# Scores from rounded parts and rests, softmax sums divided out of the rows of values, and the last layer's rows turned by DMA

## The chip, the core and the metric

The program runs on one core of a Trainium2 chip. The metric is device time in microseconds (us); lower is better. The engines are PE (TensorE, matrix products), DVE (VectorE), ACT (ScalarE), POOL (GpSimd) and SP, which here only starts transfers. Every engine takes its instructions strictly in the order in which the program lists them, and waits at the first one whose inputs or buffers are not there.

## What is computed

The reference, cut to what matters:

```
q, k, v: [4, 8, 576, 64]                      # batch, heads, rows, head size
scores = q @ k.T / 8;  keep the 32 largest of each row, others -> -1e9
attn = exp(scores - max) / (sum + 1e-9);      a = attn @ v
x = a as [2304, 512]                          # heads side by side
x = (sigmoid(x @ w_gate) * (x @ w_val)) @ w_out          # 512 -> 1536 -> 512
h = x @ w_in;  s = h * softmax(h)                        # 512 -> 1024
y = (s - mean(s)) / sqrt(var(s) + 1e-6) * g_ln @ w_out2  # 1024 -> 512
```

## The kernel before

**Chunks and steps.** The 2304 rows are handled as 18 chunks of 128 rows (16 of one batch, 2 that hold the remaining 64 rows of two batches each). A chunk has four steps, so there are 72; a step is one pair of heads (in the two remainder chunks two pairs of half the rows). The numbers behind tile names are steps or chunks: `ps40` is the score tile of step 40, `xt7` the input of chunk 7 to the layers.

**One step.** PE computes the scores in two halves of 288 keys (`scores`, L625 for the remainder, L628): fp32 products over 64 rows of the array, the two heads of the pair in the upper and the lower 64 rows. I call the instructions of one half a set: there are two sets a step. ACT takes them to SBUF (`s`, L634). DVE finds the 32nd largest value by rounds of MAX8 and MATCH_REPLACE8 (L639 to L657). ACT removes what lies below (L675) and takes the exponential with its row sum (L680). POOL and DVE make the inverse sum (L684, L688), ACT writes the normalized f16 part `h` with the inverse as a per-row scale (L701), POOL normalizes the fp32 values (`norm`, L693) and writes the f16 rest (L705). A DMA on SP's queue turns both parts (`et`, L712), and PE multiplies with the values (`attend`, tile `av`, L727).

**One chunk in the layers.** All products of the layers use three f16 terms: part by part, part by rest, rest by part. ACT writes the f16 part of the input (`xt`, L753); the rest comes either straight from DVE (`rows_direct`, L764, chunks in `DIRECT`), or by an fp32 copy on ACT and a difference on POOL (L771). PE then computes gate (`pg`) and value (`pv`, both L863), `px` (L909), `ph` (L946), after the normalization the turned rows (`pl`, L1018, eight fp32 transposes a chunk), and `po` (L1044). The part and the rest of `px` and `pl` are made as for `xt`, with `DIRECT` deciding for each chunk. The two chunks in `LATE` (16 and 17) have shorter ways at the end.

**The order.** A planner in the kernel (class `Order`) has a list of operations with engine, cost, due time, needs and buffers; due times are shifted by the table `SHIFT`. It plays the whole program once and writes out the order for every engine. Operations of different chunks and steps are thus interleaved: gate products of one chunk stand between score sets and `av` groups of later steps. At the start, weights are loaded (64-bit words from which DVE rebuilds fp32), summed, and split by ACT (L495, L496) and POOL (L499) into f16 part and rest. Buffers are counted by kind in `BUFS`: `pm` are the four PSUM tiles that all products of the layers share, `ps` the one score tile, `s` and `w` the step's SBUF tiles, `big` the two tiles for raw weights, `e` and `lt`.

Of the kernel before, what the change touches and what calls it, by code (L numbers as in the profile page):

```python
# [1189 lines left out]
```

## Time and profile before

| | |
|---|---|
| median of 3 runs | 1003.15 us (1002.62 to 1004.39) |
| the profiled execution | 1002.34 us |
| its span, first to last instruction | 1000.6 us |
| PE busy | 883.0 us, 88% |
| DVE busy | 865.0 us, 86% |
| ACT busy | 724.4 us, 72% |
| POOL busy | 569.6 us, 57% |

The profile is of one execution. The start of a PE instruction is recorded, its end is modelled, so the time a group of matmuls holds PE is read from the distance to the next group's start, and not from the duration beside it. Durations on ACT and DVE overlap their neighbours by about 0.1 us.

### The profile page before, as it was taken

The numbers are of one execution on the slowest core, as the hardware profiler recorded it, in microseconds if no ns is written. First come the engines' busy times: TensorE is split into PE (matmuls) and PEld (weight loads), VectorE is DVE, ScalarE is ACT, GpSimd is POOL, SyncE is SP. The second block draws the span as 40 slices with busy tenths as digits, with TensorE's granted clock in tenths as the row PEclk, the third lists the DMA queues.
The fourth block names the chain that finished last, engine by engine and source line by source line (L and its number), as shares of the span: only waits on it lengthen the run. The fifth ranks groups of instructions, "written<-read, shape, count | busy, mean of one in ns | idle before, by whom it ended". The sixth has DMA issues, their size and how long they took to land.

```text
span 1000.6 us, 29578 instructions
## 1 busy us (share of the span) xinstructions
PE 883.0 (88%) x12052; PEld 668.1 (67%) x12052; DVE 865.0 (86%) x2321; ACT 724.4 (72%) x1319; POOL 569.6 (57%) x824
## 2 busy tenths in 40 slices
PE   1343249899999999999999999999999999999995
PEld 1112138777786868786877777676868687877962
DVE  7999999999999999999899999999999999823232
ACT  4998999888789878667797776777987677632221
POOL 6876787786657766555475645645673546530000
PEclk9999658999999999999999999999999999999998
DMA  9982565142641433332514433334332224220000
GB/s 339 327 257 66 138 158 126 30 83 65 141 118 38 95 85 58 82 93 75 112 51 76 63 59 84 84 82 106 77 73 61 69 49 83 50 59 4 10 12 21
DMA packets 194200, 91.56 MB, mean 92 GB/s; under 512 B 171792, under 2 KB 181008, under 8 KB 194064
## 3 DMA queue, kind: packets, MB, share of 16 engines
q1 hardware_dynamic: 194064, 89.68, 36.7%
q8 instruction: 94, 1.54, 0.7%
q14 instruction: 42, 0.34, 0.1%
HBM read 42.47 MB, written 4.72 MB: 47 GB/s over the span
## 4 chain that ended last, share of the span: by engine, by line
PE 75%; DVE 13%; ACT 6%; DMA 3%; issue 1%; POOL 1%; SPq 0%; POOLq 0%; ACTq 0%; DVEq 0%
PE pg L863 15%; PE pv L863 14%; PE px L909 12%; PE ph L946 9%; PE po L1044 9%; PE ps L628 8%; PE av L727 6%; DVE m L653 3%; DVE w L657 2%; PE pl L1018 2%; DVE pd L424 1%; DMA raw<-in_w_in_dram 1%; DMA wi<-in_w_gate_dram 1%; DVE pd L427 1%; PE ps L625 1%
## 5 line engine op out<-in xcount | busy, mean ns | idle before, releaser
L653 DVE MAX8 m<-w 128x8 f32<-128x288 f32 (+1 forms) x576 | 328.6, 598 | 0.1
L657 DVE MATCH_REPLACE8 w<-m,w 128x288 f32<-128x288 f32 (+1 forms) x432 | 232.5, 542 | 0.0
L705 POOL TENSOR_TENSOR h<-s,h 128x576 f16<-128x576 f32 x144 | 184.5, 1285 | 3.1 <-POOL nk L662 0.2
L863 PE MATMUL pg<-xt,wg 128*128 128x128 f16 x2592 | 180.1, 222 | 3.2 <-POOL xt L771 2.2
L909 PE MATMUL px<-gh,wo 128*128 128x128 f16 x2592 | 177.7, 219 | 0.0
L863 PEld LDWEIGHTS <-wg 128*128 128x128 f16 x2592 | 158.1, 100 | 22.9 <-issue 12.1
L863 PE MATMUL pv<-xt,wv 128*128 128x128 f16 x2592 | 171.9, 219 | 0.1
L909 PEld LDWEIGHTS <-wo 128*128 128x128 f16 x2592 | 152.0, 98 | 23.0 <-issue 13.4
L863 PEld LDWEIGHTS <-wv 128*128 128x128 f16 x2592 | 152.5, 98 | 20.5 <-issue 9.9
L693 POOL TENSOR_SCALAR s<-s,sm 128x576 f32<-128x576 f32 x144 | 106.7, 745 | 102.2 <-ACT h L701 101.7
L628 PE MATMUL ps<-k,q 64*128 64x288 f32 x512 | 105.3, 488 | 28.9 <-ACT s L634 11.7
L634 ACT ACTIVATE s<-ps 128x576 f32<-128x576 f32 x144 | 92.6, 643 | 50.6 <-PE ps L628 38.0
L675 ACT ACTIVATE s<-s,nk 128x576 f32<-128x576 f32 x144 | 105.3, 767 | 32.5 <-POOL nk L662 32.3
L701 ACT ACTIVATE h<-s,sm 128x576 f16<-128x576 f32 x144 | 107.4, 767 | 20.4 <-DVE sm L688 16.6
L1044 PE MATMUL po<-wo,lt 128*128 128x512 f16 x432 | 119.7, 389 | 0.0
L946 PE MATMUL ph<-wi,x 128*128 128x512 f16 x432 | 119.5, 388 | 0.0
L680 ACT ACTIVATE s<-s,nb 128x576 f32<-128x576 f32 x144 | 110.0, 766 | 1.1 <-POOL nb L669 1.0
L628 PEld LDWEIGHTS ps<-k,q 64*128 64x128 f32 x512 | 42.1, 198 | 67.8 <-issue 21.4
L727 PE MATMUL av<-et,v 128*64 128x128 f16 (+1 forms) x2400 | 77.9, 220 | 6.5 <-ACT v L608 6.0
L727 PEld LDWEIGHTS <-v 128*64 128x64 f16 x2400 | 66.3, 113 | 23.9 <-issue 12.7
L639 DVE TENSOR_TENSOR w<-ps,s 128x576 f32<-128x576 f32 x72 | 54.1, 751 | 26.1 <-ACT s L634 17.5
L684 POOL TENSOR_SCALAR sm<-sm 128x2 f32<-128x2 f32 x72 | 13.8, 191 | 108.9 <-ACT s L680 103.7
(166 smaller groups left out, 1236.9 us busy)
## 6 DMA issues: line engine op xcount, KB each, us to landing
v<-in_v_pad_dram SPq DMA_DIRECT2D x16, 320.0 KB, 4.1
k<-in_k_dup_dram SPq DMA_DIRECT2D x32, 144.0 KB, 3.1
wi<-in_w_gate_dram SPq DMA_DIRECT2D x8, 512.0 KB, 6.0
q<-in_q_main_dram SPq DMA_DIRECT2D x32, 128.0 KB, 3.3
wo<-in_w_val_dram SPq DMA_DIRECT2D x8, 512.0 KB, 7.6
wi<-in_w_out_dram SPq DMA_DIRECT2D x8, 512.0 KB, 5.4
raw<-in_w_in_dram SPq DMA_DIRECT2D x8, 512.0 KB, 4.8
raw<-in_w_out_dram SPq DMA_DIRECT2D x8, 512.0 KB, 4.4
```

Source lines behind the costliest of these rows:

```text
L628: nc.tensor.matmul(ps[:, t, :S // 2], q[rows, p], kv["k", b, p][rows, keys], start=True, stop=True)
L653: nc.vector.max(st["m8"][:, t, r * 8:r * 8 + 8], ranked(i, r, t))
L657: nc.vector.match_replace(w, steps[i]["m8"][:, t, r * 8:r * 8 + 8], w, LOW)
L680: nc.scalar.activation(w, w, AF.Exp, bias=st["nb"][:, t:t + 1], scale=D ** -0.5, accum_out=st["sm"][:, t:t + 1])
L693: nc.gpsimd.tensor_scalar(w, w, st["sm"][:, t:t + 1], 1.0, op0=OP.mult, op1=OP.mult)
L701: nc.scalar.activation(st["h"][:, 0, t], st["s"][:, t], AF.Copy, scale=st["sm"][:, t:t + 1])
L705: nc.gpsimd.tensor_sub(st["h"][:, 1, t], st["s"][:, t], st["h"][:, 0, t])
L727: nc.tensor.matmul(ch["av"][j * D:(j + 1) * D, p, st["o"]:st["o"] + wd], v, e[:, y * REM:y * REM + wd], start=one and k == (0, 5)[j], stop ...
L863: nc.tensor.matmul(dst, w[a][:, c, f * P:(f + 1) * P], ch["xt"][:, b, c], start=x == 0, stop=x == len(mm) - 1)
L909: nc.tensor.matmul(ch["px"][:, e], wo1h[a][:, f, e * P:(e + 1) * P], ch["gh"][:, b, f], start=y == 0, stop=y == len(DOWN) - 1)
L946: nc.tensor.matmul(ch["ph", nn], ch["x2"][:, a, c], wih[b][:, c, nn * 512:(nn + 1) * 512], start=c == 0 and a == 0 and b == 0, stop=c == K ...
L1044: nc.tensor.matmul(ch["po"], ch["lt"][:, a, f], wo2h[b][:, f], start=y == 0, stop=y == len(FIN) - 1)
```

## The change

- **Scores.** `q` and `k` are split when loaded: a part rounded to float32r (F32R; ACT, `split_q`, `split_k`) and the rest (POOL, `rest_q`, `rest_k`). The `k` tile of one head holds the rounded part in 64 of its rows and the rest in the other 64, and `q` stands in both halves, so that one F32R product over 128 rows gives part by part and part by rest. A second F32R product over 64 rows adds rest by part. A set has four matmuls in place of two (eight in place of four in the remainder). `k` is loaded with both copies, `q` once a step and not once a chunk.
- **Softmax sums.** `h` is written from the exponentials without a scale, and `norm` is gone. The inverse sums are made once a chunk, split in two f16 parts (`inverse_halves`), spread over the array by PE (`spread`, tile `rb`, 16 matmuls a chunk, 32 in a remainder chunk), taken to SBUF by ACT (`take_spread`) and multiplied with `av` by DVE (`rows_all`). From this ACT makes the part of `xt`, POOL the rest.
- **Last layer.** For the chunks 0 to 15 ACT and POOL split the rows into part and rest (`last_hi`, `last_lo`) and one DMA turns both (`flip_last`); the PE transposes and the three ways of making `lt` from `pl` stay for chunks 16 and 17.
- **Tables.** `DIRECT` holds chunks 16 and 17 only, so the rest of `px` is made by ACT and POOL for the others. `BUFS` and `SHIFT` are new, and with them the order.

```diff
-DIRECT = tuple(range(4, 18))
+DIRECT = (16, 17)
-BUFS = dict(s=4, ks=5, v=4, q=2, w=4, et=2, ...)
+BUFS = dict(s=3, ks=8, v=4, qr=2, qs=3, w=3, et=2, ...)
     ("w", "g"): -850.7, ...
+    ("w", "g"): -600.6, ...
+    def split_q(i):
...
+        nc.scalar.activation(st["qh"], st["qr"], AF.Copy)
+    def rest_q(i):
...
+            nc.gpsimd.tensor_sub(st["ql"][rows, :n], st["qr"][rows, part], st["qh"][rows, part].bitcast(F32))
+    def split_k(b, p, j):
...
+        nc.scalar.activation(ks, kv["raw", b, p, j], AF.Copy)
+    def rest_k(b, p, j):
...
+        rows = slice(D - j * D, P - j * D)
+        nc.gpsimd.tensor_sub(ks[rows], kr[rows], ks[rows].bitcast(F32))
@@ scores
-                    nc.tensor.matmul(ps[:, t, :S // 2], q[rows, p], kv["k", b, p][rows, keys], start=True, stop=True)
+        for x, p in enumerate(st["pairs"]):
+            for t in range(2):
+                nc.tensor.matmul(ps[:, t, :S // 2], qh[:, t * num + x], kv["k", b, p, t][:, keys], start=x == 0, stop=False)
         for x, p in enumerate(st["pairs"]):
             for t in range(2):
                 rows = slice(t * D, t * D + D)
+                nc.tensor.matmul(ps[:, t, :S // 2], ql[rows, x], kv["k", b, p, t][rows, keys], start=False, stop=x == num - 1)
-    def norm(i, t):
...
+    def spread(ch):
+        ch["rb"] = rb = tl(pp, [P, NPAIR, P], F32, f"rb{ch['x']}", "pm")
+        for y, i in enumerate(ch["steps"]):
...
+                for a in range(2):
+                    for t in range(2):
+                        nc.tensor.matmul(rb[t * D:t * D + D, p, st["o"]:st["o"] + wd], ch["ih"][:, a, 2 * y + t:2 * y + t + 1].to_broadcast([P, D]),
+                                         ident16[:, rows], start=a == 0, stop=a == 1)
@@ prob_hi
-        nc.scalar.activation(st["h"][:, 0, t], st["s"][:, t], AF.Copy, scale=st["sm"][:, t:t + 1])
+        nc.scalar.activation(st["h"][:, 0, t], st["s"][:, t], AF.Copy)
+    def take_spread(ch):
...
+            nc.scalar.activation(ch["xf"][:, :, w], ch["rb"][:, :, w], AF.Copy, scale=by)
     def rows_all(ch):
+        nc.vector.tensor_mul(ch["xf"], ch["av"], ch["xf"])
     def rows_hi(ch):
+        nc.scalar.activation(ch["xt"][:, 0], ch["xf"], AF.Copy)
+    def last_hi(ch):
...
+        nc.scalar.activation(ch["lh"][:, 0], ch["e"].rearrange("p a b -> p (a b)"), AF.Copy)
+    def last_lo(ch):
+        nc.gpsimd.tensor_sub(ch["lh"][:, 1], ch["e"].rearrange("p a b -> p (a b)"), ch["lh"][:, 0])
+    def flip_last(ch):
+        nc.sync.dma_start(ch["lt"].rearrange("p c k q -> p (c k) q"), ch["lh"].rearrange("p c f -> p (c f)"), transpose=True)
```

**Where the order moves, first place.** PE in the middle of the program, before: the end of a gate group, four of the eight transposes of a chunk, a score set, and the start of an `av` group.

```order
L863 LDWEIGHTS wg_75
L863 MATMUL pg_7940<-xt7_7464,wg_75 128x128
L1018 MATMUL pl_8045<-ident_64,e_7786 128x128 x4
L628 MATMUL ps37_1_8052<-k2_1_6849,q9_0_6630 128x288 x2
L727 LDWEIGHTS v1_2_4356
L727 MATMUL av32_7565<-et34_7871,v1_2_4356 64x128
```

PE now, the same score set: its four matmuls stand between value products.

```order
L899 MATMUL pv_8571<-xt7_7872,wv_78 128x128
L647 MATMUL ps37_1_8590<-ks2_1_0_7818,qs37_7824 128x288
L647 MATMUL ps37_1_8590<-ks2_1_1_7956,qs37_7824 128x288
L651 MATMUL ps37_1_8590<-ks2_1_0_7818,qs37_7824 128x288
L651 MATMUL ps37_1_8590<-ks2_1_1_7956,qs37_7824 128x288
L899 LDWEIGHTS wv_78
```

The transposes are gone from this place, and the set has two matmuls over the whole array (L647) ahead of two over half of it (L651). Before, two fp32 instructions stand there, each of which the trace shows as two records.

**Second place.** ACT ahead of the input of chunk 1 (`xt1`), before: splitting of weights, then `xt1` straight from `av`.

```order
L496 ACTIVATE wo2_79<-wo2_79,gscale_81 128x512
L495 ACTIVATE ts_2112<-wo2_79,gscale_81 128x512
L496 ACTIVATE wo2_79<-wo2_79,gscale_81 128x512
L753 ACTIVATE xt1_2129<-av4_1737 128x512
L675 ACTIVATE s9_1730<-s9_1730,nk9_2039 128x576
```

ACT now at this place.

```order
L791 ACTIVATE xf_2263<-rb1_2154 128x512
L706 ACTIVATE s8_1925,sm8_2261<-s8_1925,nb8_2230 128x576
L738 ACTIVATE h8_2301<-s8_1925 128x576
L657 ACTIVATE s10_2307<-ps10_0_2240 128x2x288
L497 ACTIVATE ts_2320<-wo2_81,gscale_83 128x512
L498 ACTIVATE wo2_81<-wo2_81,gscale_83 128x512
L738 ACTIVATE h8_2301<-s8_1925 128x576
L798 ACTIVATE xt1_2330<-xf_2263 128x512
```

`xt1` now stands behind work of step 8 and behind the spread sums of its own chunk (`xf` from `rb1`); between that row and `xt1` DVE has to multiply.

## Rows read from the trace of the kernel before

**Rows 1.** Waits of PE from 200 to 960 us, all of them: total, times, longest

```profile
PE ps L628 <- DVE w L643: 1.1, 2, 0.8
PE ptot L385 <- ACT sq L915: 0.8, 1, 0.8
PE pg L863 <- ACT ot L1051: 0.4, 1, 0.4
PE pl L1018 <- POOL e L1013: 0.2, 1, 0.2
```

**Rows 2.** Busy time by stage: stretch, length, PE, PEld, DVE, ACT, POOL, clock, DMA

```profile
150.00:200.00 50.00, 46.37 (x714) 41.25 (x710) 48.25 (x126) 44.08 (x75) 37.74 (x50) 0.91 0.33 78
200.00:350.00 150.00, 147.75 (x2224) 112.75 (x2222) 142.87 (x405) 125.61 (x238) 105.37 (x155) 1.00 0.41 90
350.00:850.00 500.00, 499.71 (x7010) 376.89 (x7010) 476.74 (x1318) 376.15 (x703) 286.43 (x453) 1.00 0.35 76
```

**Rows 3.** Timeline of PE in two places: start, us, what, [wait]

```profile
452.98 0.84 PE L946 MATMUL ph<-wi,x 128*128 128x512 f16 x3
453.75 0.76 PE L628 MATMUL ps<-k,q 64*128 64x288 f32 x4
454.44 0.85 PE L946 MATMUL ph<-wi,x 128*128 128x512 f16 x3
...
462.69 0.84 PE L946 MATMUL ph<-wi,x 128*128 128x512 f16 x3
463.45 1.03 PE L727 MATMUL av<-et,v 128*64 128x128 f16 x30
464.42 0.85 PE L909 MATMUL px<-gh,wo 128*128 128x128 f16 x12
```

**Rows 4.** The same view around a remainder set and a gate group

```profile
243.94 0.83 PE L863 MATMUL pg<-xt,wg 128*128 128x128 f16 x12
244.70 0.72 PE L625 MATMUL ps<-k,q 64*64 64x288 f32 x8
245.35 0.84 PE L863 MATMUL pg<-xt,wg 128*128 128x128 f16 x12
246.03 0.84 PE L1044 MATMUL po<-wo,lt 128*128 128x512 f16 x3
```

**Rows 5.** The same view around four of the transposes

```profile
862.40 0.61 PE L1018 MATMUL pl<-ident,e 128*128 128x128 f32 x4
862.84 0.83 PE L863 MATMUL pg<-xt,wg 128*128 128x128 f16 x12
```

**Rows 6.** Groups of ACT, POOL and DVE: line, what, count | busy us, mean ns | idle before

```profile
L701 ACT ACTIVATE h<-s,sm 128x576 f16<-128x576 f32 x144 | 107.4, 767 | 20.4 <-DVE sm L688 16.6 <-issue 2.4 <-ACT s L634 0.9
L894 ACT ACTIVATE gh<-sg 128x512 f16<-128x512 f32 x54 | 32.3, 621 | 19.1 <-DVE sg L889 18.8
L693 POOL TENSOR_SCALAR s<-s,sm 128x576 f32<-128x576 f32 x144 | 106.7, 745 | 102.2 <-ACT h L701 101.7
L705 POOL TENSOR_TENSOR h<-s,h 128x576 f16<-128x576 f32 x144 | 184.5, 1285 | 3.1 <-POOL nk L662 0.2
L764 DVE SCALAR_TENSOR_TENSOR lt<-pl,lt 128x512 f16<-128x512 f32 x28 | 19.0, 683 | 25.0 <-ACT lt L1023 25.0
```

**Rows 7.** Chain that ended last, where chunk 0 enters the layers: start, us, what

```profile
145.07 0.43 ACT xt L753
...
150.70 7.16 PE pg L863 x84
```

**Rows 8.** The same view, where chunk 1 enters

```profile
188.17 0.88 ACT wo L496
189.05 0.44 ACT xt L753
...
190.72 1.16 POOL xt L771
...
191.93 3.10 PE pg L863 x38
```

More of the change, by code (lines that the diff above doesn't have):

```diff
@@ L11 @@
 F32 = mybir.dt.float32
+F32R = mybir.dt.float32r
 F16 = mybir.dt.float16
@@ L44 @@
 V_DOWN = 11
-BUFS = dict(s=4, ks=5, v=4, q=2, w=4, et=2, ps=1, pt=1, av=1, pm=4, xt=1, gh=1, two=3, big=2, xf=1, x2=1)
+BUFS = dict(s=3, ks=8, v=4, qr=2, qs=3, w=3, et=2, ps=1, pt=1, av=1, pm=4, xt=1, gh=1, two=3, big=2, xf=1, x2=1)
 STEP = 12.0
@@ L173 @@
                 POOL=(100, 70, 80, 100, 1250), DMA=(0,) * 5)
-    TAKER = dict(s="ACT", ks="DMA", v="DMA", q="DMA", w="DVE", et="DMA", ps="PE", pt="PE", av="PE", pm="PE",
+    TAKER = dict(s="ACT", ks="ACT", v="DMA", qr="DMA", qs="ACT", w="DVE", et="DMA", ps="PE", pt="PE", av="PE", pm="PE",
                  xt="ACT", gh="ACT", two="ACT", big="DMA", xf="ACT", x2="ACT")
@@ L538, in weights @@
             W = (key, f, c)
-            add(("wh", *W), "ACT", 1.48, t + 0.6 * x, lambda f=f, c=c: split_hi(f, c), [("wc", key)], take=["two"])
+            add(("wh", *W), "ACT", 1.44, t + 0.6 * x, lambda f=f, c=c: split_hi(f, c), [("wc", key)], take=["two"])
             add(("wl", *W), "POOL", 1.23, t + 0.6 * x, lambda f=f, c=c: split_lo(f, c), [("wh", *W)], free=["two"])
@@ L572, in body @@
         ch["x"] = x
+        ch["steps"] = [i for i, st in enumerate(steps) if st["ch"] is ch]
     kv = {}
@@ L576, in body, with load_q, load_k @@
     vstat = cp.tile([P, B * NPAIR], F32, name="vstat")
-    def load_q(ch, j):
-        ch["q", j] = qt = tl(sp, [P, NPAIR, P], F32, f"q{ch['x']}_{j}", "q")
-        b = ch["vs"][j]
+    def load_q(i):
+        st = steps[i]
+        if st["rem"]:
+            st["qr"] = tl(sp, [P, 4, P], F32, f"qr{i}", "two")
+            nc.sync.dma_start(st["qr"], q_rem[st["b"], st["c"]])
+        else:
+            st["qr"] = tl(sp, [P, 2, P], F32, f"qr{i}", "qr")
+            p = 2 * st["pairs"][0]
+            nc.sync.dma_start(st["qr"], q_main[st["b"], st["c"], :, p:p + 2])
+    def split_q(i):
+        st = steps[i]
+        st["ql"] = qs = tl(sp, [P, 3, P], F32R, f"qs{i}", "qs")
+        st["qh"] = tl(sp, [P, 4, P], F32R, f"qh{i}", "two") if st["rem"] else qs[:, 1:]
+        nc.scalar.activation(st["qh"], st["qr"], AF.Copy)
+    def rest_q(i):
+        st = steps[i]
+        n = len(st["pairs"])
         for t in range(2):
             rows = slice(t * D, t * D + D)
-            if ch["rem"]:
-                nc.sync.dma_start(qt[rows].rearrange("d (h x) q -> d h x q", h=2),
-                                  q_rem[b, :, rows, 2 * t:2 * t + 2].rearrange("h d x q -> d h x q"))
-            else:
-                nc.sync.dma_start(qt[rows], q_main[b, ch["c"], rows].rearrange("d (p j) q -> d p j q", j=2)[:, :, t])
-    def load_k(b, p):
-        kv["k", b, p] = kt = tl(sp, [P, S], F32, f"k{b}_{p}", "ks")
-        for t in range(2):
-            nc.sync.dma_start(kt[t * D:t * D + D], k_dup[b, 2 * p + t, t * D:t * D + D])
+            part = slice(t * n, t * n + n)
+            nc.gpsimd.tensor_sub(st["ql"][rows, :n], st["qr"][rows, part], st["qh"][rows, part].bitcast(F32))
+    def load_k(b, p, j):
+        kv["raw", b, p, j] = kr = tl(sp, [P, S], F32, f"kr{b}_{p}_{j}", "big")
+        nc.sync.dma_start(kr, k_dup[b, 2 * p + j])
+    def split_k(b, p, j):
+        kv["k", b, p, j] = ks = tl(sp, [P, S], F32R, f"ks{b}_{p}_{j}", "ks")
+        nc.scalar.activation(ks, kv["raw", b, p, j], AF.Copy)
+    def rest_k(b, p, j):
+        kr, ks = kv["raw", b, p, j], kv["k", b, p, j]
+        rows = slice(D - j * D, P - j * D)
+        nc.gpsimd.tensor_sub(ks[rows], kr[rows], ks[rows].bitcast(F32))
     def load_v(b, p):
@@ L778, in body @@
         t = use[0] * STEP
-        add(("kd", b, p), "DMA", 1.0, t - 3 * STEP, lambda b=b, p=p: load_k(b, p),
-            ([("kd", b, p - 1)] if p else [("kd", b - 1, NPAIR - 1)] if b else []), take=["ks"], delay=0.95)
+        for j in range(2):
+            add(("kd", b, p, j), "DMA", 0.85, t - 3 * STEP, lambda b=b, p=p, j=j: load_k(b, p, j),
+                ([("qk", uses[b - 1, p][-1], 1)] if b else []) + [("kd", b, p, 0)] * j, take=["big"], delay=0.95)
+            add(("kb", b, p, j), "ACT", 0.575, t - 2 * STEP,
+                lambda b=b, p=p, j=j: split_k(b, p, j), [("kd", b, p, j)], take=["ks"])
+            add(("ka", b, p, j), "POOL", 1.37, t - 2 * STEP, lambda b=b, p=p, j=j: rest_k(b, p, j),
+                [("kb", b, p, j)], free=["big"])
         add(("vd", b, p), "DMA", 0.91, t - STEP, lambda b=b, p=p: load_v(b, p), take=["v"], delay=0.95)
@@ L786, in body @@
             add(("vl", b, p, x), "POOL", 0.75, t + STEP, lambda b=b, p=p, x=x: value_lo(b, p, x), [("vh", b, p, x)], free=["two"])
-    for x, ch in enumerate(chunks):
-        ch["steps"] = [i for i, st in enumerate(steps) if st["ch"] is ch]
-        for j in range(len(ch["vs"])):
-            add(("qd", x, j), "DMA", 0.8, ch["steps"][2 * j] * STEP - 3 * STEP, lambda ch=ch, j=j: load_q(ch, j),
-                [("qd", x, j - 1) if j else ("qd", x - 1, len(chunks[x - 1]["vs"]) - 1)] if x or j else [], take=["q"], delay=0.95)
     for i, st in enumerate(steps):
@@ L795, in body @@
         rem, b, ch = st["rem"], st["b"], st["ch"]
-        done_q = st["last"] or rem and ch["steps"].index(i) == 1
+        add(("qd", i), "DMA", 0.8 if rem else 0.5, t0 - 3 * STEP, lambda i=i: load_q(i), [("qd", i - 1)] * (i > 0) + [("qk", i - 1, 1)] * rem,
+            take=["two" if rem else "qr"], delay=0.95)
+        add(("qb", i), "ACT", 0.52 if rem else 0.31, t0 - 2 * STEP, lambda i=i: split_q(i), [("qd", i)] + [("qb", i - 1)] * (i > 0),
+            take=["qs"] + ["two"] * rem)
+        add(("qa", i), "POOL", 1.4 if rem else 0.78, t0 - 2 * STEP, lambda i=i: rest_q(i), [("qb", i)], free=["two" if rem else "qr"])
         for n in range(2):
-            add(("qk", i, n), "PE", 0.5, t0 - STEP, lambda i=i, n=n: scores(i, n),
-                [("qd", ch["x"], st["j"])] + [("kd", b, p) for p in st["pairs"]] + ([("qk", i, 0)] if n else [("qk", i - 1, 1)] if i else []), take=["ps"],
-                free=(["q"] * done_q + ["ks"] * sum(uses[b, p][-1] == i for p in st["pairs"])) * n)
-            add(("se", i, n), "ACT", 0.53, t0 - STEP, lambda i=i, n=n: take_scores(i, n), [("qk", i, n)] + [("se", i, 0)] * n,
+            add(("qk", i, n), "PE", 0.95 if rem else 0.5, t0 - STEP, lambda i=i, n=n: scores(i, n),
+                [("qa", i)] + [("ka", b, p, t) for p in st["pairs"] for t in range(2)] + ([("qk", i, 0)] if n else [("qk", i - 1, 1)] if i else []),
+                take=["ps"], free=(["qs"] + ["two"] * rem + ["ks"] * sum(2 * (uses[b, p][-1] == i) for p in st["pairs"])) * n)
+            add(("se", i, n), "ACT", 0.55, t0 - STEP, lambda i=i, n=n: take_scores(i, n), [("qk", i, n)] + [("se", i, 0)] * n,
                 take=["s"] * (n == 0), free=["ps"] * (n == 0))
@@ L820, in body @@
         for t in range(2):
[L821 removed]
+            add(("be", i, t), "ACT", 0.68, e, lambda i=i, t=t: below(i, t), [("nk", i), ("se", i, 1)])
             add(("ex", i, t), "ACT", 0.76, e, lambda i=i, t=t: expo(i, t), [("be", i, t), ("nb", i)])
[L823 to L824 removed]
         for t in range(2):
[L826 to L828 removed]
+            add(("hh", i, t), "ACT", 0.6, e, lambda i=i, t=t: prob_hi(i, t), [("ex", i, t)] + [("hh", i, 0)] * t + [("hh", i - 1, 0)] * (t == 0 and i > 0), take=["w"] * (t == 0))
+            add(("hl", i, t), "POOL", 1.28, e, lambda i=i, t=t: prob_lo(i, t), [("hh", i, t)] + [("hl", i, 0)] * t,
                 free=["s"] * t)
[L830 removed]
+        add(("tr", i), "DMA", 3.5, e + 3, lambda i=i: flip_halves(i), [("hl", i, 1)] + [("tr", i - 1)] * (i > 0), take=["et"], free=["w"], delay=1.5,
             room=lambda i=i: room_halves(i))
@@ L849, in body @@
                     needs.append(("vk", key, bb))
-            cost = 0.57 if len(ch["vs"]) == 1 else 0.8
-            add(("xh", ch["x"]), "ACT", cost, e + 6, lambda ch=ch: rows_hi(ch), needs, take=["xt"])
-            if ch["x"] in DIRECT:
-                add(("xl", ch["x"]), "DVE", 0.6 if len(ch["vs"]) == 1 else 0.75, e + 6, lambda ch=ch: rows_direct(ch), [("xh", ch["x"])], free=["av"])
-            else:
-                add(("xf", ch["x"]), "ACT", cost, e + 6, lambda ch=ch: rows_all(ch), [("xh", ch["x"])], take=["xf"], free=["av"])
-                add(("xl", ch["x"]), "POOL", 1.11, e + 6, lambda ch=ch: rows_rest(ch), [("xf", ch["x"])], free=["xf"])
+            x = ch["x"]
+            add(("iw", x), "POOL", 0.19, e, lambda ch=ch: total1(ch), [("ex", y, t) for y in ch["steps"] for t in range(2)])
+            add(("iv", x), "DVE", 0.08, e, lambda ch=ch: inverse(ch), [("iw", x)])
+            add(("ih", x), "POOL", 0.36, e, lambda ch=ch: inverse_halves(ch), [("iv", x)])
+            add(("rb", x), "PE", 0.46, e + 5, lambda ch=ch: spread(ch), [("ih", x)] + ([("va", x - 1, 7)] if x else []), take=["pm"])
+            add(("rs", x), "ACT", 0.5 if len(ch["vs"]) == 1 else 0.7, e + 5, lambda ch=ch: take_spread(ch), needs[1:] + [("rb", x)], take=["xf"], free=["pm"])
+            add(("xa", x), "DVE", 0.61, e + 6, lambda ch=ch: rows_all(ch), [("at", i), ("rs", x)], free=["av"])
+            add(("xh", x), "ACT", 0.52, e + 6, lambda ch=ch: rows_hi(ch), [("xa", x)], take=["xt"])
+            add(("xl", x), "POOL", 1.12, e + 6, lambda ch=ch: rows_rest(ch), [("xh", x)], free=["xf"])
     def group(ch, dst, w, f):
@@ L1063, in tA, with op @@
             return (4 * x + BEHIND + 4 * a / ATOMS) * STEP
-        def op(name, engine, cost, a, fn, needs=(), take=(), free=(), table=None, delay=0.0, x=x, port=None):
-            add((*name[:1], x, *name[1:]), engine, cost, tA(a), fn, needs, take, free, table, delay, port)
+        def op(name, engine, cost, a, fn, needs=(), take=(), free=(), table=None, delay=0.0, x=x, port=None, room=None):
+            add((*name[:1], x, *name[1:]), engine, cost, tA(a), fn, needs, take, free, table, delay, port, room)
         if ("fs", key) not in order.ops:
@@ L1119, in body @@
         N = ATOMS
-        for nn in range(2):
+        if x not in LATE:
+            op(("lh",), "ACT", 0.95, 57, lambda ch=ch: last_hi(ch), [("l4", x)], take=["w"])
+            op(("ll",), "POOL", 2.3, 57, lambda ch=ch: last_lo(ch), [("lh", x)], free=["big"])
+            op(("lr",), "DMA", 3.1, N + 10, lambda ch=ch: flip_last(ch), [("ll", x)], take=["big"], free=["w"], delay=1.5,
+               room=lambda ch=ch: room_last(ch))
+        for nn in range(2) if x in LATE else ():
             op(("tu", nn), "PE", 0.455, N + 22, lambda ch=ch, nn=nn: turn(ch, nn), [("l4", x)], take=["pm"],
```

69 lines of the change are left out of this document (31 added, 38 removed), and 137 rows, old and new, of the table SHIFT.

## The prediction

> **What bounds the kernel now.** I read the waits of PE first. From 200 to 960 us PE waited for other engines four times, 2.5 us in all [rows 1]. So in that stretch the time is the sum of what PE has to do. The stages beside it [rows 2] show how little that says about the others: from 350 to 850 us DVE is busy 476.7 of 500 us (95%), ACT 376.2 (75%), POOL 286.4 (57%), and yet none of them is waited for. From 150 to 200 us it is different: PE is busy only 46.4 of 50 us, ACT 44.1, DVE 48.3. In the chain [rows 7, 8] the first gate product of chunk 0 starts at 150.70 after ACT's `xt`, and that of chunk 1 at 191.93, after ACT has split weights until it comes to `xt` at 189.05. So the program is: start until 150.7, ACT in front of chunk 1, then PE alone until the last chunk. A saving of PE counts in full; a saving of DVE counts for nothing as long as PE is not waiting; more work on ACT counts in the first 200 us, and later only if it eats ACT's idle quarter.
>
> **PE's prices.** What a group holds is read from starts. A group of 1536 f16 columns (12 matmuls of 128, 3 of 512) holds PE 0.68 us (245.35 to 246.03, [rows 4]), so 128 columns cost 0.057 and 288 columns 0.127. A score set: 452.98 to 453.75 is 0.77, 0.09 more than the group ahead of it needs, and 453.75 to 454.44 is 0.69 [rows 3]; the set costs 0.78. Four fp32 transposes cost 0.44, 0.11 each with its own weights [rows 5], that is 0.25 for 288 fp32 columns. The trace counts four records a set, two upper, two lower, side by side; two of 0.25 one after the other make 0.50, and 0.28 is left for entering and leaving the half-array form. An `av` group of 30 matmuls in 15 side-by-side pairs costs 0.08 ahead plus 0.97 [rows 3], 1.05; 15 x 0.057 leave 0.20 for entering and leaving.
>
> **The change on PE.**
> - Sets, 128 of them in the main steps: two full-array matmuls and one side-by-side pair, 3 x 0.127 + 0.28 = 0.66 against 0.78, so -0.12 x 128 = -15.4 us. Here is the one open price: no row shows an F32R matmul. Below it is bounded by the f16 rate, 0.127, above by the fp32 rate, 0.25 for 288 columns. I take 0.127, since an f16 operand and a rounded one are both a single part, and the two records of fp32 are what several parts cost. By "FP8 and Floating Point Precision" of the Trainium skill (TensorE Precision Notes) full fp32 is four products of halves; one of four would be an estimated 0.125 and move the sum by 1 us.
> - Remainder sets, 16: now 0.09 + 0.65 = 0.74 (243.94 to 244.70 to 245.35, [rows 4]); then four full ones and two pairs, 6 x 0.127 + 0.28 = 1.04. +0.30 x 16 = +4.8 us.
> - Transposes of 16 chunks: 128 x 0.11 = -14.1 us.
> - `rb`: 16 matmuls, 8 pairs, 8 x 0.057 + 0.20 = 0.66 for 16 chunks; at most twice that for the two remainders, I take 0.75. +12.0 us.
>
> Sum -12.7 us. Some sets stand directly behind one another before and pay the way in once, which gives back about 1. Of what is left some 2.5 fall before the first gate, where PE waits anyway: the sets of the first steps are in the order of either kernel ahead of it. **On the path: -9 us.**
>
> **The other engines.** DVE loses 24 differences for `lt`, 12 for `px`, about 14 for `xt` at 0.68 each [rows 6] and most reciprocals, and gains 18 multiplications: about -30 us, worth nothing by rows 1, but it gives DVE room. POOL loses `norm`, 144 x 0.745, and gains the rests of `q`, `k`, `xt`, `px` and the last rows, about as many elements, but as differences (1.285 for 576 against 0.745, [rows 6]): some +50 us on an engine with 43% idle. ACT gains the roundings of `q` (64 of 256 elements) and `k` (32 of 576), the last layer's part and more copies of `px`; it loses the copies of `pl` and the per-row scale of `h`. From 0.621 for 512 elements [rows 6] I estimate 0.33 for 256 and 0.70 for 576 without the scale, against 0.767 with it: about +45 us in all, 2.5 a chunk. In 350 to 850 us that fits into the idle quarter. A wait is added on SP: the turning of the last rows waits for POOL, and behind it in SP's queue stand loads of `q` and `k` and the turning of later steps' `h`. What is late then is an `av` group; the planner keeps these some us ahead of PE, and I give it 1 us together with the tighter last step, whose score set is now about 24 us of PE work ahead of its `av` group, where it was 32.
>
> **The start.** Ahead of `xt0` ACT's queue now has 8 roundings of `q` (2.6), 8 of `k` (5.6) and one spread copy (0.6) more, and two exponentials, two removals, one `h` and two pieces of weight splitting less, with the cheaper `h` about 6: +2.8, and with 0.1 us of overlap for each of the net 10 instructions +1.8. After `xt` the way is shorter: 145.07 to 150.70 now has a second copy in a queue; then it is ACT 0.62, POOL 1.16 [rows 8] and three hand-overs, about 2.3 against 5.6. First gate: 150.7 + 1.8 - 3.3 = 149.2.
>
> **Chunk 1.** Ahead of `xt1` the same count gives +13.4 us (12 roundings of `q`, 8 of `k`, four instructions of one more step, three on `px` of chunk 0, the rest cancels), less overlap for 27 instructions: +10.7. The way from `xt1` to the gate is 0.6 shorter. ACT's idle time in 150 to 200 us, 5.9 us [rows 2], can take some of it or none: gate of chunk 1 between 191.93 + 10.7 - 0.6 - 5.9 = 196.1 and 202.0, I take 199.5. PE would be there at 149.2 + 41.5 (its work by these prices up to there, 35 before) + 3.8 (the same excess as before, 189.5 less 150.7 less 35) = 194.5. So PE waits 5 us, and ACT decides.
>
> **The sum.** From chunk 1's gate to the end the trace has 1000.6 - 191.9 = 808.7 us. Of PE's work 6.5 us have moved in front and 9 are gone: 808.7 - 15.5 = 793.2. End: 199.5 + 793.2 + 2 (SP, the last step, ACT now and then) = 994.7. The profiled execution took 1.7 us more than its span, and lies 0.8 below the median: **997 us**, about 0.5% faster than 1002.3.
>
> **Rivals.**
> - *ACT stays late.* Up to `xt4` ACT's queue grows by about 16 us. If its idle time (24 of 150 us from 200 to 350, [rows 2]) lies where ACT waits for others and none of it is taken up, chunk 4 comes 16 us late, and the 15.5 us that PE saves behind are eaten: 1000.6 + 0.5 + 2 + 1.7 = 1005, with more such places up to 1012. It decides from the point where PE waits over 10 us in front of chunks 1 to 4. For it: ACT is in the chain at both entries [rows 7, 8]. Against: from chunk 2 on ACT is not waited for [rows 1]. 0.23.
> - *The weights of the rounded matmuls load in the open.* A load of 128 fp32 columns takes at most the 0.11 of a transpose [rows 5]; 320 full-array matmuls x 0.11 = +35 us: 1032. At the fp32 rate the 480 places of a matmul or pair would cost 0.12 more, +58: 1050 with ACT's wait gone. For it: no row shows F32R. Against: transposes with their own fp32 weights follow every 0.11, less than one 0.127. The Trainium skill says in "TensorE: Matmul & The Clock Gate" (Part 3, what overlaps and what doesn't) that a weight load overlaps a running matmul only when the row group differs; by that rule 1032. The trace disagrees for f16: twelve matmuls, each with its own weights for the same rows, hold PE 0.68 us [rows 4]; no run here shows it for F32R. 0.10.
> - *DVE sets the pace after all*, 95% busy as it is, and PE's order only follows: then its -30 us count, 972 to 985. Against: rows 1. 0.10.
>
> **How the numbers follow.** Forecast 0.57, around 997, by itself 988 to 1004 (ACT's idle time taken up or not, +-3; a step of 0.02 in the F32R matmul, +-8; SP and the order). The others as given. The range leaves out the slow matmuls and half of the DVE case: 984 to 1012. A measurement here can tell about 0.2%, 2 us, from no change. Faster: 0.70 of the forecast and the DVE case, 0.50; same: 0.16, from the forecast's upper end and the lower end of the ACT case; slower: 0.34.
>
> **What would show it.** PE's score set: starts 0.66 us apart from the group behind it beyond its own lead (right), near 0.9 (open loads) or over 1.0 (fp32 rate). No `pl` before chunk 16; `rb` groups of 0.66. First gate near 149, chunk 1's gate near 199 with PE waiting for POOL or ACT `xt`. From 250 to 950 us PE's waits under 10 us, DVE down to about 90%, ACT up to about 83%. Wrong it is if PE waits for ACT or SP all along, or if a set costs more than 0.75.

## The result, and the profile after

The changed kernel takes 1009.9 us (median of six runs, 1007.1 to 1013.5), the kernel before 1003.6 beside it: a ratio of 1.0063, 95% interval 1.0039 to 1.0087. It is 0.6% slower, where I had forecast 0.5% faster. The profiled execution took 1010.25 us, its span 1008.5.

Waits of PE from 200 to 965 us in the changed kernel, which answer to [rows 1] (total, times, longest):

```profile
PE po L1093 <- DVE sg L925: 1.9, 1, 1.9
PE ps L647 <- ACT s L657: 1.6, 4, 1.1
PE px L945 <- POOL gh L933: 1.5, 2, 0.9
PE ps L647 <- DVE w L666: 1.3, 3, 0.6
PE ps L647 <- DVE n L374: 0.8, 1, 0.8
```

They were 2.5 us in all; now the five longest alone are 7.1. The stages, in the columns of [rows 2]:

```profile
150.00:200.00 50.00, 42.36 (x590) 34.41 (x588) 48.44 (x128) 43.15 (x77) 35.20 (x50) 0.94 0.29 79
200.00:350.00 150.00, 146.20 (x2304) 121.80 (x2303) 132.56 (x367) 126.58 (x247) 106.89 (x151) 1.00 0.51 108
350.00:850.00 500.00, 495.62 (x7022) 388.40 (x7023) 444.65 (x1209) 385.73 (x749) 320.75 (x473) 1.00 0.45 97
```

From 350 to 850 us DVE is busy 32 us less and is at 89%, ACT is at 77%, POOL at 64%. No engine is full, and still PE is busy 4 us less in that stretch than before. The timeline of PE shows the sets, a main one, a remainder one, and the spread sums `rb` (to compare with [rows 3, 4]):

```profile
601.77 0.83 PE L899 MATMUL pv<-xt,wv 128*128 128x128 f16 x12
602.41 0.51 PE L647 MATMUL ps<-ks,qs 128*128 128x288 f32 x2
602.85 0.40 PE L651 MATMUL ps<-ks,qs 64*128 64x288 f32 x2
603.18 0.85 PE L982 MATMUL ph<-wi,x 128*128 128x512 f16 x3
...
250.75 0.83 PE L899 MATMUL pv<-xt,wv 128*128 128x128 f16 x12
251.40 0.77 PE L647 MATMUL ps<-ks,qh 128*128 128x288 f32 x4
252.09 0.53 PE L651 MATMUL ps<-ks,qs 64*128 64x288 f32 x4
252.56 2.18 PE L899 MATMUL pv<-xt,wv 128*128 128x128 f16 x36
...
235.51 0.85 PE L1093 MATMUL po<-wo,lt 128*128 128x512 f16 x3
236.29 0.64 PE L729 MATMUL rb<-ident,ih 128*64 128x128 f16 x16
236.86 0.85 PE L1093 MATMUL po<-wo,lt 128*128 128x512 f16 x3
```

From the group ahead to the group behind, less the group ahead's 0.67 or 0.68: the main set costs 603.18 - 601.77 - 0.67 = 0.74, where I had put 0.66 and the kernel before has 0.78. The two full-array matmuls take 602.85 - 602.41 = 0.44, 0.22 each, where I had put 0.127. The remainder set costs 252.56 - 250.75 - 0.67 = 1.14 (I had 1.04). `rb` costs 236.86 - 235.51 - 0.68 = 0.67 (I had 0.66). The first gate (`pg`) with the score set ahead of it on PE, before and now, and the gate of chunk 1 now:

```profile
149.37 1.33 PE L628 MATMUL ps<-k,q 64*128 64x288 f32 x4 [1.88 <-ACT s L634]
150.63 1.68 PE L863 MATMUL pg<-xt,wg 128*128 128x128 f16 x14
...
142.82 0.82 PE L647 MATMUL ps<-ks,qs 128*128 128x288 f32 x2 [3.12 <-DVE w L666]
143.57 0.61 PE L651 MATMUL ps<-ks,qs 64*128 64x288 f32 x2
144.11 2.10 PE L899 MATMUL pg<-xt,wg 128*128 128x128 f16 x18
...
196.14 0.22 PE L899 MATMUL pg<-xt,wg 128*128 128x128 f16 x1 [0.92 <-ACT xt L798]
197.57 1.33 PE L899 MATMUL pg<-xt,wg 128*128 128x128 f16 x11 [1.21 <-POOL xt L804]
```

The first gate starts at 144.1 (forecast 149.2), the run of chunk 1's gate behind the rest of `xt1` at 197.6 (forecast 199.5). From there to the end it is 810.9 us, where [rows 8] left 808.7 and I had 793.2 + 2. In both kernels the first gate follows at once on a score set that waited, before for ACT's `s`, now for DVE's `w`; [rows 7] leaves out the pieces of the chain in which this set stands.

**A balance of PE.** For all kernels below I took each group's distance to the next group's start and took off its price: 0.0565 for 128 f16 columns, 0.2265 for 512, 0.11 for a transpose, and for sets, `av` and `rb` the medians of undisturbed ones. What is left I call waiting; it is a remainder and also takes up errors of the prices (0.01 in the price of a set makes 1.4 us), and the profile's own view of PE's waits names less of it (2.5 us before and 7.9 now, in the stretches shown above). So differences between lines are to be read, and those under 2 us are not. The balance runs from the first gate to the start of PE's last group; 8.8 us of the last column are one wait near the end, for the rows of the last chunk. The kernels of the experiments stand in it already; times are medians, and the kernel before took 1002.1 to 1003.6 beside each of them.

| kernel | time | first gate | work of PE | waiting to chunk 1's first gate matmul | then to 850 us | behind |
|---|---|---|---|---|---|---|
| before | 1003.6 | 150.6 | 821.3 | 4.6 | 4.8 | 9.3 |
| changed | 1009.9 | 144.1 | 821.9 | 10.2 | 13.6 | 8.9 |
| keys split once (e3) | 1006.5 | 142.6 | 821.9 | 10.7 | 10.5 | 8.9 |
| f16 sets (e1) | 996.9 | 142.5 | 799.7 | 11.9 | 20.8 | 9.1 |
| f16, four `s` (e13) | 995.4 | 142.1 | 799.7 | 11.7 | 21.3 | 9.1 |
| f16, four `w` (e14) | 984.7 | 142.6 | 799.7 | 10.3 | 10.3 | 9.3 |
| f16, four of both (e4) | 984.9 | 142.1 | 799.7 | 10.3 | 10.6 | 9.2 |
| f16 and load (e7) | 1006.5 | 143.2 | 821.9 | 10.9 | 11.0 | 9.0 |
| f16 and load, four of both (e8) | 999.5 | 140.9 | 821.9 | 9.4 | 3.6 | 9.1 |

The two upper lines hold the result: the program gets to the layers 6.5 us earlier, PE's work is the same to 0.6 us instead of some 9 less, and PE waits 14 us more.

### The profile page after: what moved, and what is told of

It reads as the page before. It is cut to its first block, busy times and chain, and to the rows that moved or that the text cites. A ratio compares the mean times of both kernels' runs of the same rounds, so it can differ in the third digit from the quotient of the medians.

```text
span 1008.5 us, 30356 instructions
## 1 busy us (share of the span) xinstructions
PE 889.6 (88%) x12244; PEld 698.4 (69%) x12244; DVE 846.7 (84%) x2234; ACT 757.4 (75%) x1425; POOL 630.6 (63%) x872
## 4 chain that ended last, share of the span: by engine, by line
PE 55%; DVE 7%; ACT 6%; POOL 1%; DMA 1%; issue 1%; POOLq 0%; DVEq 0%; ACTq 0%
PE pv L899 10%; PE pg L899 10%; PE px L945 10%; PE po L1093 8%; PE ph L982 7%; PE av L764 4%; PE ps L647 3%; PE ps L651 3%; DVE m L676 2%; DVE w L680 2%; DMA et<-h 1%; ACT v L632 1%; ACT s L706 1%; ACT s L697 1%; DVE w L662 1%
## 5 line engine op out<-in xcount | busy, mean ns | idle before, releaser
L899 PE MATMUL pg<-xt,wg 128*128 128x128 f16 x2592 | 172.7, 221 | 3.1 <-POOL xt L804 1.2
L899 PEld LDWEIGHTS <-wv 128*128 128x128 f16 x2592 | 151.9, 98 | 14.1 <-issue 0.9
L899 PEld LDWEIGHTS <-wg 128*128 128x128 f16 x2592 | 152.7, 99 | 10.2 <-issue 4.8
L647 PE MATMUL ps<-ks,qs 128*128 128x288 f32 x256 | 74.9, 374 | 37.2 <-ACT s L657 19.6
L662 DVE TENSOR_TENSOR w<-ps,s 128x576 f32<-128x576 f32 x72 | 54.3, 753 | 62.2 <-ACT s L657 23.0
L738 ACT ACTIVATE h<-s 128x576 f16<-128x576 f32 x144 | 96.1, 673 | 2.4 <-DMA lt<-lh 2.3
L647 PEld LDWEIGHTS ps<-ks,qs 128*128 128x128 f32 x256 | 44.1, 205 | 52.4 <-ACT s L657 24.2
L603 POOL TENSOR_TENSOR qs<-qr,qs 64x128 fp32r<-64x128 f32 x128 | 58.1, 454 | 17.1 <-ACT qs L595 11.5
L1093 PEld LDWEIGHTS <-lt 128*128 128x128 f16 x432 | 38.4, 97 | 40.7 <-issue 4.0
```

The source lines that it names most:

```text
L647: nc.tensor.matmul(ps[:, t, :S // 2], qh[:, t * num + x], kv["k", b, p, t][:, keys], start=x == 0, stop=False)
L738: nc.scalar.activation(st["h"][:, 0, t], st["s"][:, t], AF.Copy)
L899: nc.tensor.matmul(dst, w[a][:, c, f * P:(f + 1) * P], ch["xt"][:, b, c], start=x == 0, stop=x == len(mm) - 1)
L1093: nc.tensor.matmul(ch["po"], ch["lt"][:, a, f], wo2h[b][:, f], start=y == 0, stop=y == len(FIN) - 1)
```

## Experiments

**The price of a set.** In e1 the parts and rests of `q` and `k` are f16; no engine's order changes.

```diff
-        st["ql"] = qs = tl(sp, [P, 3, P], F32R, f"qs{i}", "qs")
+        st["ql"] = qs = tl(sp, [P, 3, P], F16, f"qs{i}", "qs")
-        kv["k", b, p, j] = ks = tl(sp, [P, S], F32R, f"ks{b}_{p}_{j}", "ks")
+        kv["k", b, p, j] = ks = tl(sp, [P, S], F16, f"ks{b}_{p}_{j}", "ks")
```

> The changed kernel with f16 in place of F32R for the parts and rests of q and k; the order of all engines is the same row by row. In the trace of the changed kernel a main score set takes 0.74 us of PE and a remainder set 1.14, where the prediction had 0.66 and 1.04 from the f16 rate. Theory 1, the F32R matmuls themselves are what was mis-sized: the sets fall to 0.66 and 1.04, 128 x 0.08 + 16 x 0.10 = 11.8 us of PE, of which about 1 lies ahead of the first gate: 1009.9 - 10.7 = about 999. Theory 2, the other engines set the pace from 200 us on: the sets get shorter, PE waits by as much longer, and the time stays within 3 us of 1009.9. Theory 3, the form of the set (full-array matmuls, then a half-array pair) costs the time and not the type: the sets stay at 0.74.

Measured: 996.9 us, ratio 0.9943 (0.9930 to 0.9955). A set in the timeline of e1:

```profile
371.32 0.83 PE L945 MATMUL px<-gh,wo 128*128 128x128 f16 x12
371.99 0.41 PE L647 MATMUL ps<-ks,qs 128*128 128x288 f16 x2
372.33 0.30 PE L651 MATMUL ps<-ks,qs 64*128 64x288 f16 x2
372.56 0.85 PE L945 MATMUL px<-gh,wo 128*128 128x128 f16 x12
```

The set costs 372.56 - 371.32 - 0.67 = 0.57, 0.17 less than with F32R and less than the 0.66 expected; the remainder sets fell from 1.14 to 0.94. Theory 1 holds, with more than it asked for, and theory 3 falls. But 22.2 us less work gave only 13.0 us: waiting between chunk 1's gate and 850 us rose from 13.6 to 20.8. So something else stands close behind PE. That 996.9 is also the time I had forecast is chance: the sets are cheaper than I assumed, and the waiting is larger.

In e2 the full-array matmuls of each first half take 384 columns instead of 288.

```diff
+                wide = slice(0, 384) if n == 0 else keys
-                nc.tensor.matmul(ps[:, t, :S // 2], qh[:, t * num + x], kv["k", b, p, t][:, keys], start=x == 0, stop=False)
+                nc.tensor.matmul(ps[:, t, :wide.stop - wide.start], qh[:, t * num + x], kv["k", b, p, t][:, wide], start=x == 0, stop=False)
```

> The changed kernel, with 384 columns in place of 288 in the full-array F32R matmuls of the first half of each step (96 columns more than are used), nothing else. In the changed kernel one such matmul holds PE 0.22 us. If that is a weight load of about 0.095 in the open and then the f16 rate of 0.44 ns a column, it becomes 0.264 (+0.042). If F32R runs at 0.77 ns a column and loads are hidden, it becomes 0.295 (+0.074). The whole would get about 64 x 2 x 0.042 + 8 x 4 x 0.042 = 6.7 us longer by the first, 12 us by the second, if PE is the bound.

The timeline of e2, a wide set and a narrow one:

```profile
371.06 0.83 PE L946 MATMUL px<-gh,wo 128*128 128x128 f16 x12
371.70 0.59 PE L648 MATMUL ps<-ks,qs 128*128 128x384 f32 x2
372.21 0.40 PE L652 MATMUL ps<-ks,qs 64*128 64x288 f32 x2
372.54 0.84 PE L946 MATMUL px<-gh,wo 128*128 128x128 f16 x12
...
375.64 0.83 PE L946 MATMUL px<-gh,wo 128*128 128x128 f16 x12
376.28 0.51 PE L648 MATMUL ps<-ks,qs 128*128 128x288 f32 x2
376.72 0.40 PE L652 MATMUL ps<-ks,qs 64*128 64x288 f32 x2
377.05 0.84 PE L946 MATMUL px<-gh,wo 128*128 128x128 f16 x12
```

Two wide matmuls take 0.51, two narrow ones 0.44. From single starts, median of 88 pairs, and of 176 in the changed kernel, one takes 0.258, against 0.217: 0.041 for 96 columns, 0.43 ns a column, which is the f16 rate (0.0565 for 128 is 0.44). What does not grow with the columns is 0.217 - 288 x 0.00043 = 0.094. So by these two widths the F32R matmul streams as fast as f16, and each takes 0.094 us more that does not grow. With f16 the same two full-array matmuls, each with its own weights, start 0.122 apart, and the 0.094 is gone.

That it is the load of the weights fits, but is not shown by itself. The trace has rows for the loads: those of the changed kernel, of e1, and of the transposes before, on which the prediction leaned (behind the first bar: busy us, mean ns of one).

```profile
L647 PEld LDWEIGHTS ps<-ks,qs 128*128 128x128 f32 x210 | 33.6, 190 | 11.5 <-issue 3.3 <-ACT s L657 3.0
...
L647 PEld LDWEIGHTS <-qs 128*128 128x128 f16 x210 | 17.0, 99 | 19.0 <-issue 5.8 <-DVE w L666 4.4 <-DVE n L374 1.4
...
L1018 PEld LDWEIGHTS pl<-ident,e 128*128 128x128 f32 x144 | 16.1, 146 | 12.0 <-issue 9.6 <-POOL e L1013 0.7 <-DVE e L1010 0.5
```

An F32R load is listed with 0.190 us, an f16 load with 0.099, so the difference, 0.091, is near the 0.094. The row of the second load begins 0.083 us after the start of the first matmul in both widths (medians), so loads are listed beside a running matmul for F32R too, and yet the longer stream of e2 hides no more of it. Whether the 0.094 is half of a longer load, or another fixed cost of F32R, no run separates; two F32R matmuls on the same weights would. The time of e2, 1013.07 in its only run, is 3.2 above 1009.9, less than the 6.7 expected from PE's sum, and within the spread of the changed kernel's runs, so it decides nothing.

The Trainium skill, "TensorE: Matmul & The Clock Gate", section "LDWEIGHTS (loading the stationary operand)", gives a load of 128 columns as 128 / 1.2 = 107 ns; the f16 rows above, 99 ns, are near it, the F32R rows, 190 ns, are not. The rule in Part 3 of that page of the Trainium skill, that a load overlaps a running matmul only when the row group differs, does not describe the f16 matmuls here, whose loads for the same rows are hidden; the 0.094 of F32R would fit it.

**Who makes PE wait.** In e3 only the first pair's keys are split and all steps use them, which takes 30 roundings from ACT and 30 differences from POOL.

```diff
     def split_k(b, p, j):
+        if (b, p) != (0, 0):
+            kv["k", b, p, j] = kv["k", 0, 0, j]
+            return
     def rest_k(b, p, j):
+        if (b, p) != (0, 0):
+            return
```

> The changed kernel, but only the keys of the first pair of heads are split; all steps use these (the scores of the other heads are left out). The order of everything else is the same. It takes 30 roundings of 0.6 us from ACT and 30 differences of 1.38 us from POOL; PE's work is the same. Theory A, ACT and POOL are late with the split of the keys and what stands behind it, and that is where PE's waiting after chunk 1's gate comes from (about 8 us between 196 and 850 us that the kernel before does not have): the waiting goes, and six roundings less ahead of the first gates bring some 3 more, 998 to 1001. Theory B, the waiting comes from elsewhere (three tiles of s and w in place of four, the longer way from the sums to xt): only the start gets shorter, 1005 to 1008.

Measured: 1006.5 us, ratio 1.0040 (1.0027 to 1.0054), a time that theory B has. 15 us less busy time on ACT and 40 less on POOL (sums of its stages against those of the changed kernel) bring 3.4 us, 1.5 of it at the first gate; between chunk 1's gate and 850 us the waiting falls by 3.1 of 13.6. So the gain is not at the start alone, as theory B had it, but most of the added waiting stays.

In e4 the f16 kernel has four tiles of `s` and `w`, in the old order.

```diff
-        return pool.tile(shape, dtype, name=name, tag=tag, bufs=bufs or BUFS[tag])
+        return pool.tile(shape, dtype, name=name, tag=tag, bufs=bufs or dict(BUFS, s=4, w=4)[tag])
```

> The f16 kernel of the run beside it, with four tiles each of s and w where the changed kernel has three (the f16 keys leave the room); the order of all engines is the same, only waits for a free tile can end earlier. If the three tiles cause PE's waiting after chunk 1's gate, it is 4 to 8 us faster than the f16 kernel with three, else within 1.5 us of it.

Measured: 984.9 us, ratio 0.9827 (0.9812 to 0.9842): 12 us faster than e1, more than expected, with the same instructions in the same order. The waiting up to 850 us halves, from 20.8 to 10.6. Which of the two tiles it is, e13 (`s=4`) and e14 (`w=4`) tell.

> The f16 kernel (996.9), four tiles of s (a step's scores and exponentials) and three of w (the copy that the top-k works on, and the part and rest h). Same order. Four of both gave 984.9. If the s tile is the tight one (held from the first score set until POOL has written the rest), nearly all of the 12 us come here, 985 to 988; if it is w, 994 to 997.

> The same with three tiles of s and four of w. If w is the tight one (held by the top-k and then by h until the DMA has turned it), 985 to 988; if it is s, 994 to 997. If both runs lie in the middle, both are needed.

Measured: 995.4 (ratio 0.9923, 0.9905 to 0.9941) and 984.7 (0.9815, 0.9798 to 0.9832). With f16 it is `w` alone. The waits of DVE at L662 from 196 to 850 us in the changed kernel show how:

```profile
DVE w L662 <- ACT s L657: 14.5, 15, 5.1
DVE w L662 <- PE ps L651: 13.6, 8, 4.8
...
DVE w L662 <- DMA et<-h: 5.8, 3, 3.1
...
DVE w L662 <- DMA lt<-lh: 1.3, 1, 1.3
```

Those of ACT in the same stretch, at the instructions that take a `w`:

```profile
ACT lh L1053 <- POOL e L1049: 5.6, 6, 1.8
...
ACT lh L1053 <- DMA et<-h: 2.9, 1, 2.9
...
ACT h L738 <- DMA lt<-lh: 2.3, 2, 1.2
```

`DVE w` at L662 starts the top-k of a step. It needs nothing of the DMA that turns an earlier step's `h`, except its tile: the copy for the top-k, `h`, and now also the last layer's `lh` all come out of the kind `w`. Before there were four tiles for two users, now there are three for three, and each `h` and `lh` holds its tile until POOL has written the rest and the DMA has turned it. How much of it is the third user and how much the missing tile was not separated. These waits on a DMA are 12 us in sum for ACT and DVE. The waits to compare with e14 are those of e1, which differs from it in the tile alone (DVE, then ACT, then PE):

```profile
DVE w L662 <- PE ps L651: 10.0, 7, 4.4
...
DVE w L662 <- DMA et<-h: 4.2, 2, 3.0
...
ACT lh L1053 <- DMA et<-h: 3.3, 2, 2.9
...
ACT h L738 <- DMA lt<-lh: 2.3, 2, 1.2
...
PE ps L647 <- ACT s L657: 4.2, 5, 1.6
PE ps L647 <- DVE w L666: 2.4, 6, 0.7
```

In e14 neither DVE nor ACT waits for one of these two DMAs any more, and what is left of the other rows is:

```profile
DVE w L662 <- PE ps L651: 6.8, 5, 4.5
...
PE ps L647 <- ACT s L657: 2.2, 2, 1.5
...
PE ps L647 <- DVE w L666: 1.0, 2, 0.7
```

So without the tile ACT and DVE are put back, and come late for PE's score sets.

**The same at the F32R price.** No run has a fourth `w` beside F32R keys; it is the f16 keys that left the room for it. So e7 and e8 give the f16 set the length of the F32R one by three short matmuls into unused columns (four in the remainder), e7 with three tiles, e8 with four of both.

```diff
+        for x in range(4 if st["rem"] else 3):
+            nc.tensor.matmul(ps[:, x % 2, 384:512], qh[:, x % 2], kv["k", b, st["pairs"][0], x % 2][:, :128], start=True, stop=True)
```

> The f16 kernel with three tiles of s and w, and ahead of each score set three (remainder: four) more f16 matmuls of 128 columns into an unused part of the score tile, so that a set holds PE as long as with F32R: 0.57 + 3 x 0.057 = 0.74, remainder 0.94 + 4 x 0.057 = 1.17. The order is the same. It is the control for the run with four tiles beside it: if the F32R price of a set is all that separates the f16 kernel (996.9) from the changed kernel (1009.9), it gives 1009 to 1011; if F32R does something else to the program, less.

> The same with four tiles of s and w and the same order. Theory 1, the three tiles are what lets PE wait in the changed kernel (8 us more from 196 to 850 us than before): then 1000 to 1004. Theory 2, at the F32R price PE is late enough that three tiles do, and the waiting comes from the order and the loads of ACT: then within 2 us of the control, 1008 to 1011.

Measured: e7 1006.5 (ratio 1.0033, 1.0020 to 1.0046), e8 999.5 (0.9953, 0.9937 to 0.9968). The control came out 3 us under the changed kernel; the intervals of the two ratios overlap, and I leave that remainder open. Against the control the four tiles of both bring 7.0 us, as theory 1 has it, and the waiting up to 850 us falls from 11.0 to 3.6, below the 4.8 of the kernel before.

**Undoing the other parts.** e10 turns the last rows on PE again, e11 divides the sums out in each step again, both on top of e4. Each takes operations away and so gets a new order from the planner.

```diff
# e10
-        if x not in LATE:
+        if False:
             op(("lh",), "ACT", 0.95, 57, lambda ch=ch: last_hi(ch), [("l4", x)], take=["w"])
...
-        for nn in range(2) if x in LATE else ():
+        for nn in range(2):
# e11
-        nc.scalar.activation(st["h"][:, 0, t], st["s"][:, t], AF.Copy)
+        nc.scalar.activation(st["h"][:, 0, t], st["s"][:, t], AF.Copy, scale=st["sm"][:, t:t + 1])
```

> The f16 kernel with four tiles (984.9), the last layer's rows turned on PE again, as in the kernel before (128 transposes in 16 chunks, part by ACT, rest by DVE from chunk 4 on); raw keys have a tile of their own. The planner makes a new order. If the term of the prediction holds (128 x 0.11 = 14.1 us of PE on the path, turning by DMA hidden), 998 to 1000. If the DMA turning made waits of its own, less: 990 to 995.

> The f16 kernel with four tiles (984.9), the softmax sums divided out in every step again, as in the kernel before (per-row scale in h, norm on POOL, xt straight from av, its rest by DVE from chunk 4 on). No rb on PE. The planner makes a new order. If only PE's sum counts, the 12 us of rb go: 973. If the step's way through POOL counts (144 x 0.745 us more there, and the wait for the inverse in every step), that eats the 12: 983 to 992.

Measured: 1025.0 and 1069.5, far outside both expectations. e9 shows that these two tell little of the parts: it has the instructions of e4, and differs only in that the planner knows of the four tiles (`BUFS` itself says `s=4`, `w=4`) and plays a new order from the old table.

> The f16 kernel with four tiles of s and w that the planner knows of too, so that it makes a new order with the old table of shifts. If the new order uses the tiles as well as the old one does, 980 to 988; if the table is tuned to the old order, it is slower than that, 990 to 1030. With the two runs that undo a part (1025, 1070) it shows what a new order alone costs.

Measured: 1010.2 (ratio 1.0068, 1.0042 to 1.0094), 25 us more than e4 for an order that the table of shifts was not made for. So what the two undone parts are worth by themselves stays open. Their prices on PE are read from the trace (0.67 for `rb`, no `pl` up to chunk 15); what they do to the other engines was not separated.

**A last try.** e12 is e4 with two tiles of `xf`.

> The f16 kernel with four tiles of s and w (984.9) and two of xf, which hold the spread sums, the rows of values, the fp32 copy of px and some scratch. Same order. If the chain through xf (spread sums, product, part, rest) delays ACT and POOL, 2 to 4 us less; if PE's work and the start are all that is left, within 1 us.

Measured: 983.6 (ratio 0.9809, 0.9792 to 0.9826), the fastest of all, though 1.3 us from e4 is hardly more than runs differ, and lies between the two expectations, so it decides neither. By the ratios e4 and e12 are 1.7% and 1.9% faster than the kernel before, and both are about 2.5% faster than the changed one.

## Why the prediction was wrong

**The open price, F32R: wrong.** "I take 0.127, since an f16 operand and a rounded one are both a single part" was the step. One part it is, and it streams at the f16 rate; but each costs a fixed 0.094 more, most likely of its weights, so a full-array matmul holds PE 0.217. I had this as a rival and gave it 0.10, arguing from fp32 transposes that follow one another every 0.11, less than a matmul of 0.127. That row did not carry the argument: a transpose is another instruction, with 128 columns, its loads are listed with 0.146 us and those of F32R with 0.190, and no row showed what the weights of a rounded matmul do under a running one. The rival's own sum, +35 us, was wrong too. The 0.28 that I carried over from the fp32 set "for entering and leaving the half-array form" held, as I now read it, already one fixed 0.09 of this kind (two fp32 pairs follow one another after 0.34, of which 0.25 are columns), beside 0.093 for entering and 0.10 for leaving. (With f16, from single starts, an `av` group begins 0.149 after the last full-array matmul of 0.0565, the second full-array matmul of a set to the pair is 0.218 and the pair to the next group 0.225, against 0.122 a matmul.) In the F32R set no entering is seen beside the fixed part: the second full-array matmul to the pair is 0.22, as the first to the second. So a main set came to 0.74: 2 x 0.22, 0.33 for the pair, less 0.03 by which the first one starts early. With f16 it is 3 x 0.122 + 0.10 + 0.10 = 0.57, as measured.

The term by itself: 128 x -0.04 instead of -0.12, 16 x +0.40 instead of +0.30, that is 10 + 1.6 = 11.8 us with the second decimals kept. With -14.1 and +12.0 for the two other parts (no transposes up to chunk 15, and `rb` at 0.67), PE's sum is about -1 instead of -12.7. So the whole change does nothing for PE.

**The tiles: missing.** The sum has no term for `BUFS`. It stood in the change that `s` and `w` went down to three, and in the kernel that `lh` takes a `w`; I saw the tighter last step and gave 1 us for it and SP's queue together. The rows showed no wait for a tile, but they were of a kernel with four. At the F32R price four tiles of both are worth 7 us (e7 to e8; which of the two it is was not run there), with f16 sets the fourth `w` alone 12 (e1 to e14). This is the second half of the miss: from chunk 1's gate on PE has 780.0 us of work, where 787.1 of before less my 15.5 make 771.6, that is 8.4 more; and it waits 22.5 us, 8.4 more than the kernel before, where I had allowed 2.

**ACT's rival: the right time for the wrong reason.** 1009.9 lies in the 1005 to 1012 that I gave to "ACT stays late". But e8 has the same work on ACT in the same order as its control, and behind chunk 1's gate it waits no more than the kernel before; and e3, with 30 roundings less on ACT, brings 3.4 us. ACT's load has a share of that size, not more. The mechanism is one that I had not listed.

**"A saving of PE counts in full": only while nothing stands close behind.** In e1, 22.2 us of work less gave 13.0. With four tiles, e8 to e4, the same 22.2 gave 14.6. PE had hardly a wait before, and I took that for a distance. It only says that the others came in time, not by how much. ([rows 1] has five waits, where I wrote four, and two of them, 1.2 us, are on ACT, though I wrote that from chunk 2 on it is not waited for.) The rival that DVE sets the pace falls: DVE got 18 us less work over the whole run, and the time rose.

**The start: the forecast was near by luck.** The first gate came at 144.1, 5.1 us ahead of the 149.2 forecast, and not by the sum I had. I had ACT's queue ahead of `xt0` 1.8 us longer; `xt0` starts at 141.6, where it was 144.9 before. ACT is busy for 121.1 us up to there, against 120.2, but idle for 20.5 us, against 24.7: I had priced the queue as if it were packed. The way from `xt0` to the gate took the forecast length, 2.5 us against 2.3, but what PE waits for there is the score set ahead of the gate (142.82 and 149.37 above), and both parts of `xt` are there 0.3 to 0.4 us before the gate in either kernel. Why ACT idles less was not followed. At chunk 1's gate 1.9 of the 5.1 us are left (197.6 against 199.5), and they made the miss smaller. PE waits 10.2 us on the way there, where I had 3.8 + 5; of these, 2.1 stand at the gate itself, for ACT's and POOL's `xt` as I had it, where I had 5.

**Right:** `rb` at 0.67; chunk 1's gate waiting for `xt`; DVE at 89% from 350 to 850 us against "about 90%", and ACT at 77% against "about 83%". Over the whole run DVE's busy time fell by 18 us where I had 30, ACT's rose by 33 where I had 45, and POOL's by 61 where I had 50. My marks for the set, 0.66, 0.9 or 1.0, had none for the 0.74 that came; that alone should have shown me that the sum of the set was not understood.

## What to carry to other kernels

Price a new kind of matmul in two parts, what grows with its columns and what does not, and where no row shows the second part, keep both of its values and say which engine form each stands for, rather than infer it from another instruction. Where a change cuts the number of tiles or lets a new user into a kind of tile, count holders and how long each holds one, and give it a term of its own, since a trace without waits for a tile does not say how near they are. Where an order is played from a tuned table, test a part by changes that leave the order as it is (another type, a tile more, dummy work), because a new order alone cost 25 us here.
